# Both down layers of a fused kernel: seven block products in place of eight

## The chip, the cores and the metric

The kernel runs on one core of a Trainium2 chip. Its time is the device time in microseconds (us), the median of three runs. TensorE (PE in the profile) multiplies, with its weight loads (PEld) beside it; VectorE (DVE), ScalarE (ACT) and GpSimd (POOL) do the elementwise work; SyncE (SP) issues the DMAs. A weight is kept as a high and a low fp32r part (two numbers whose sum is the fp32 value), so one block product over one tile of 128 rows is three matmuls: high by high, low by high, high by low.

## The reference, cut to what matters

```python
def _moe2_ref(x, w1, w2, w3, w_out):
    a = x @ w1                  # 1792 x 1024, x is 1792 x 768
    b = x @ w2
    h = a * b @ w3              # w3: 1024 x 1024
    return h @ w_out            # w_out: 1024 x 768

def reference(...):
    attn_out = sigmoid attention  # 4 batches, 12 heads, 448 x 64
    x = attn_out as 1792 x 768
    x = _moe_ref(x, ...)          # RMS norm, SiLU gate: 768 -> 1536 -> 768
    return _moe2_ref(x, w1, w2, w3, w_out)
```

## The kernel before, in words

The kernel works on the four batches of 448 tokens; a matmul has 128x128 weights and 448 token columns. The last quarter of its program is what matters here. It goes through these stages, `g` being a pair of batches: gate layer of pair 1 (`a_winograd`), first down layer of pair 1 (`b_units(1)`), then for pair 0 and for pair 1 the product layer (`c_winograd`, `a * b`) and the last down layer (`d_units`). The weights of the last down layer, `w3 @ w_out`, were multiplied together early in the program (`w3o_group`) and lie in DRAM as `w3o`, eight row tiles of 128 x 768.

**The product layer** computes `x @ w1` and `x @ w2` for both batches of a pair with seven block products in place of eight: `winograd` (L531). The right-hand blocks are seven combinations `w0` to `w6` of the layer's input, made by `right_blocks` (L497): four subtractions on DVE, then for each of the seven blocks a rounding copy on ACT and a subtraction on DVE (`split2`, L319). `y_blocks` (L523) loads four input tiles (`ys`) from DRAM and makes the seven blocks of one of three slices k. The left-hand blocks are made for each m by `winograd_blocks` (L159): four DVE subtractions of 128x384, of which the last (L170) and the next set's first (L166) wait for POOL to have read the buffer `s`; then `split_weight` makes the two parts of each block with an ACT copy (L131) and a POOL subtraction (L134). Blocks lie in a ring of four `ws` tiles, two blocks each. Each of the seven products of an m is nine matmuls (three slices, three runs) into one of four PSUM banks (`ps_w`), and DVE adds it to the others: L548 frees the bank of product 1, L550 that of product 2, and so on; product 0's is freed by an ACT copy (L546). Bank j is needed again four products later. For each of the eight m and both batches, `c_winograd` (L573) multiplies the two results on DVE (L575) and splits the product (`ab`).

**The last down layer** (`d_group`, L627) has 12 groups for each pair (six m, two batches); a group sums 24 matmuls (eight row tiles, three runs) in a bank of `ps_m`, ACT copies it out (L631) and SP stores it (L632). Its weights come as twelve `wf` tiles of 128x512 with one ACT copy and one POOL subtraction each. Beside pair 0's groups three `y_blocks(1, k)` run for pair 1's product layer, the last of them after the eighth of twelve groups.

A scheduler fixes the order of the instructions on each engine; each engine runs its own list in that order, so a waiting instruction holds all behind it on its engine.

Of the kernel before, what the change touches and what calls it, by code (L numbers as in the profile page):

```python
# [44 lines left out]
def fused_kernel(ctx: ExitStack, tc: tile.TileContext, qkv, wg, wv, wo, w1, w2, w3, wo2, gam, out):  # L45
# [90 lines left out]
    class Weights:  # L136
# [13 lines left out]

        def add_winograd(self, srcs):

            first = len(self.seq)
            for n in range(len(srcs) * 7 // 2):
                m = [(2 * n + j) // 7 for j in range(2) if (2 * n + j) % 7 == 0]
                self.add(srcs[m[0]] if m else None, None)
            return first

        def winograd_blocks(self):  # L159

            while True:
                f = self.loaded.pop(0)
                a11, a12, a21, a22 = (f[:, j, k * WH : (k + 1) * WH] for j in range(2) for k in range(2))
                s = wp.tile([P, WT], F32, tag="mag", bufs=1, name="s")
                s1, s2 = s[:, :WH], s[:, WH:]
# [12 lines left out]
        def load_to(self, n):  # L178
            while self.n_load <= min(n, len(self.seq) - 1):
                src, kt, double, keep, use = self.seq[self.n_load]  # L180
                t = None
                if src is not None:
                    if self.out == 2:
                        return
                    self.out += 1
                    if kt is None:
                        t = wp.tile([P, 2, WT], F32, tag="wd", bufs=2, name="wd")
                        for j in range(2):
                            nc.sync.dma_start(out=t[:, j, :].rearrange("p (k c) -> p k c", c=P), in_=src[j])
                        self.loaded.append(t)  # L190
                    elif double:
                        t = load_double(src, kt)
                    else:
                        t = wp.tile([P, WT], F32, tag="wf", bufs=2, name="wf")
                        nc.sync.dma_start(out=t[:, : kt * P].rearrange("p (k c) -> p k c", c=P), in_=src)
                self.raw[self.n_load] = t
                self.n_load += 1

        def split_to(self, n):

            n = min(n, len(self.seq) - 1)
            while self.n_split <= n and len(self.split) < self.BUFS:
# [3 lines left out]
                f = self.raw.pop(i)  # L206
                w = WT if kt is None else kt * P
                if double:
# [11 lines left out]
                if kt is None:  # L220
# [35 lines left out]

    def add_d():
        return [
            [W.add(w3o[4 * h : 4 * h + 4, :, m * P : (m + 1) * P].rearrange("k p c -> p k c"), 4) for h in range(2)]
            for m in range(KD)  # L260
        ]

# [31 lines left out]
    i_c = add_gated(("w1", "w2"), KF2, 2)  # L294
    i_d = add_d()
    i_c2 = add_gated(("w1", "w2"), KF2)
    i_d2 = add_d()

# [42 lines left out]
    NH = DM // 2  # L341

    def w3o_group(kt, nh):
        ps = psm()[:, :NH]
# [5 lines left out]
        nc.scalar.activation(o, ps, AF.Copy)  # L350
        nc.sync.dma_start(out=w3o[kt, :, nh * NH : (nh + 1) * NH], in_=o)

# [77 lines left out]
    def take_out(p):  # L430
# [65 lines left out]

    def right_blocks(k, b11, b12, b21, b22):  # L497

        tt = nc.vector.tensor_tensor

        def put(j, bl, src):
            t = acts["w", j, k] = right_tile(f"w{j}", bl)
            split2(t, src)
# [19 lines left out]
    def y_blocks(g, k):  # L523
        y = []
        for m in (k, k + 3):
            for b in range(2):
                y.append(scratch("ys"))
                nc.sync.dma_start(out=y[-1], in_=yd.pop((g, b, m)))
        right_blocks(k, *y)

    def winograd(first, m, done):  # L531

        tt = nc.vector.tensor_tensor

        def product(j):
            n = 7 * (m % 2) + j
            i = first[m // 2] + n // 2
            t = W.get(i)[:, :, n % 2 * WH : (n % 2 + 1) * WH]
            ps = ps_w.tile([P, 512], F32, tag="w", bufs=4, name="w")[:, :S]
            runs(ps, t, 0, [acts["w", j, k] for k in range(3)], True, True)  # L540
            W.split_to(i + 3)
            return ps

        u, v, c11, c21 = (scratch(n) for n in ("u", "v", "c11", "c21"))
# [18 lines left out]
    def a_winograd(m):  # L563
# [7 lines left out]
        winograd(i_a2, m, done)  # L571

    def c_winograd(first, m):  # L573
# [52 lines left out]

    def d_group(g, m, b):  # L627
        t = [(W.get(i), 4) for i in (i_d2 if g else i_d)[m]]
        ps = accumulate(t, [acts["ab", b, k] for k in range(KF2)])
        o = scratch("o")  # L630
        nc.scalar.activation(o, ps, AF.Copy)  # L631
        nc.sync.dma_start(out=out[m * P : (m + 1) * P, (2 * g + b) * S : (2 * g + b + 1) * S], in_=o)  # L632

    def a_units():
# [10 lines left out]
    def d_units(g):  # L645
        for m in range(KD):
            for b in range(2):
                yield 4.5, (lambda m=m, b=b: d_group(g, m, b)), (i_d2 if g else i_d)[m][1]

# [182 lines left out]
```

## Time and profile before

| | us |
|---|---|
| median of three runs (1090.33 to 1092.02) | 1091.6 |
| profiled execution | 1088.77 |
| its span, first to last instruction | 1086.8 |
| product layer, pair 0 (from 760.21) | 102.8 |
| last down layer, pair 0 (from 863.03) | 58.8 |
| product layer, pair 1 (from 921.87) | 102.7 |
| last down layer, pair 1 (from 1024.57, its matmuls) | 58.7 |

The span is what the instructions cover; some 2 us of the execution lie around it. The stages are read off TensorE's own timeline, where one row covers a run of like matmuls; a stage's length is the distance from its first matmul to that of the next stage.

### The profile page before, as it was taken

Reading aid. Unit: us, or ns where it says so; the run is one execution under the profiler, and the core shown is the slowest. Engines: PE = TensorE matmul, PEld = TensorE weight load, DVE = VectorE, ACT = ScalarE, POOL = GpSimd, SP = SyncE. Lnnn points to the kernel's source line nnn. Section 1 sums busy time; section 2 is a strip of 40 time slices with the busy share of each in tenths; the row PEclk is TensorE's granted clock in tenths of the full one; section 3 lists DMA queues with packets and bytes.
Section 4 is the critical chain, followed back from the end, with each engine's and each line's share of the span. In section 5 each row is a group of like instructions: output and inputs, shape, how many; then the busy total and the mean of one; then the engine's idle time right before and its main releaser. Section 6 shows DMA issues by size and latency. Waiting matters only on the chain.

```text
span 1086.8 us, 13929 instructions
## 1 busy us (share of the span) xinstructions
PE 1069.4 (98%) x5152; PEld 900.2 (83%) x5152; DVE 776.9 (71%) x1018; ACT 390.2 (36%) x708; POOL 469.3 (43%) x382
## 2 busy tenths in 40 slices
PE   9999899998999999999999999999999999999998
PEld 4338799996766676799999999999999999999997
DVE  5998998999456578569787778677787635787500
ACT  5673211112244333214544443133433244333221
POOL 2646254443223323333656554223665434656420
PEclk9999899999999999999999999999999999999999
DMA  7733455575345367663221113766311244210131
GB/s 255 259 132 117 143 177 181 181 270 177 124 160 172 111 247 254 228 225 123 78 82 62 59 59 102 263 243 207 100 64 59 68 159 130 80 59 30 48 101 51
DMA packets 60980, 153.22 MB, mean 141 GB/s; under 512 B 5872, under 2 KB 32624, under 8 KB 60912
## 3 DMA queue, kind: packets, MB, share of 16 engines
q1 hardware_dynamic: 60912, 152.33, 41.7%
q8 instruction: 41, 0.67, 0.3%
q14 instruction: 27, 0.22, 0.1%
HBM read 114.95 MB, written 37.36 MB: 140 GB/s over the span
## 4 chain that ended last, share of the span: by engine, by line
PE 70%; DVE 5%; DMA 3%; ACT 1%; issue 0%; POOL 0%; SPq 0%; DVEq 0%; ACTq 0%
PE w L307 32%; PE psm L307 32%; PE av L414 2%; PE sc L396 1%; DMA raw<-in_qkv 1%; DVE mag L112 1%; PE psm L384 1%; PE av L410 1%; DVE wf L121 1%; DVE wf L124 1%; DVE mag L111 1%; PE psm L396 1%; DMA wd<-in_wg 1%; DVE wf L113 0%; DMA wd<-in_wv 0%; DMA wd<-in_wo 0%
## 5 line engine op out<-in xcount | busy, mean ns | idle before, releaser
L307 PE MATMUL w<-w,ws 128*128 128x448 f32 x1764 | 360.4, 366 | 0.1
L307 PEld LDWEIGHTS w<-w,ws 128*128 128x128 f32 x1764 | 331.2, 188 | 28.8 <-DVE c L550 0.5
L134 POOL TENSOR_TENSOR ws<-wf,ws 128x768 fp32r<-128x768 f32 (+1 forms) x88 | 153.3, 1743 | 133.8 <-ACT ws L131 129.5
L307 PE MATMUL psm<-hm,ws 128*128 128x448 f32 x864 | 178.1, 367 | 0.0
L307 PEld LDWEIGHTS psm<-hm,ws 128*128 128x128 f32 x864 | 162.0, 188 | 16.8 <-issue 1.7
L134 POOL TENSOR_TENSOR ws<-wd,ws 128x384 fp32r<-128x384 f32 x112 | 123.9, 1118 | 102.7 <-ACT ws L131 93.9
L307 PE MATMUL psm<-x,ws 128*128 128x448 f32 x648 | 140.4, 376 | 6.2 <-POOL ws L133 5.1
L307 PEld LDWEIGHTS psm<-x,ws 128*128 128x128 f32 x648 | 124.0, 193 | 24.0 <-POOL ws L133 5.5
L134 POOL TENSOR_TENSOR ws<-s,ws 128x384 fp32r<-128x384 f32 x84 | 94.8, 1136 | 67.6 <-ACT ws L131 67.6
L133 POOL CAST ws<-wf 128x768 fp32r<-128x768 f32 (+1 forms) x52 | 45.2, 869 | 180.8 <-PE psm L307 85.8
L307 PE MATMUL psm<-ab,ws 128*128 128x448 f32 x576 | 117.7, 366 | 0.0
L307 PEld LDWEIGHTS psm<-ab,ws 128*128 128x128 f32 x576 | 108.2, 188 | 9.2
L121 DVE SCALAR_TENSOR_TENSOR wf<-wd,wf 128x768 uint32<-128x768 uint32 (+1 forms) x76 | 90.2, 1186 | 2.5
L113 DVE TENSOR_SCALAR wf<-mag 128x768 uint32<-128x768 uint32 (+1 forms) x76 | 66.3, 872 | 34.6 <-POOL ws L134 30.6
L111 DVE TENSOR_SCALAR mag<-wd 128x768 uint32<-128x768 uint32 (+1 forms) x76 | 55.7, 733 | 36.8 <-DMA wd<-in_wo 22.6
L131 ACT ACTIVATE ws<-wd 128x384 fp32r<-128x384 f32 x112 | 54.8, 515 | 71.2 <-PE w L307 48.0
L124 DVE SCALAR_TENSOR_TENSOR wf<-wd,wf 128x768 uint32<-128x768 uint32 (+1 forms) x76 | 74.2, 976 | 1.5
L307 PE MATMUL psm<-o,ws 128*128 128x384 f32 x384 | 68.8, 339 | 0.0
L307 PEld LDWEIGHTS psm<-o,ws 128*128 128x128 f32 x384 | 67.4, 188 | 1.2 <-issue 1.1
L112 DVE TENSOR_SCALAR mag<-mag 128x768 f32<-128x768 f32 (+1 forms) x76 | 66.5, 874 | 1.7
L321 ACT ACTIVATE hm<-s 128x448 fp32r<-128x448 f32 x48 | 27.6, 576 | 93.3 <-DVE s L606 70.7
L414 PE MATMUL av<-a,raw 128*64 128x448 f32 x288 | 59.4, 548 | 0.0
(96 smaller groups left out, 1124.5 us busy)
## 6 DMA issues: line engine op xcount, KB each, us to landing
raw<-in_qkv SPq DMA_DIRECT2D x23, 736.0 KB, 5.8
wd<-in_wo SPq DMA_DIRECT2D x20, 768.0 KB, 6.1
wd<-in_w SPq DMA_DIRECT2D x16, 768.0 KB, 5.2
wd<-w SPq DMA_DIRECT2D x32, 384.0 KB, 3.6
wd<-in_wg SPq DMA_DIRECT2D x12, 768.0 KB, 4.5
wd<-in_wv SPq DMA_DIRECT2D x12, 768.0 KB, 4.8
wd<-in_w SPq DMA_DIRECT2D x16, 512.0 KB, 4.3
w<-wf SPq DMA_DIRECT2D x16, 384.0 KB, 2.7
```

The costliest lines, as they stand in the source:

```text
L111: nc.vector.tensor_scalar(out=mag.bitcast(U32), in0=hi, scalar1=0x7FFFFFFF, scalar2=None, op0=ALU.bitwise_and)
L112: nc.vector.tensor_scalar(out=mag, in0=mag, scalar1=HI_MIN, scalar2=HI_MAX, op0=ALU.max, op1=ALU.min)
L113: nc.vector.tensor_scalar(out=u, in0=mag.bitcast(U32), scalar1=3, scalar2=0x3FFFFFFF, op0=ALU.logical_shift_left, op1=ALU.bitwise_and,)
L121: nc.vector.scalar_tensor_tensor(out=u, in0=hi, scalar=0xC0000000, in1=u, op0=ALU.bitwise_and, op1=ALU.bitwise_or)
L124: nc.vector.scalar_tensor_tensor(out=u, in0=lo, scalar=29, in1=u, op0=ALU.logical_shift_right, op1=ALU.bitwise_or)
L131: nc.scalar.activation(t[:, 0, :w], f[:, :w], AF.Copy)
L133: nc.gpsimd.tensor_copy(out=t[:, 0, :w], in_=f[:, :w])
L134: nc.gpsimd.tensor_tensor(out=t[:, 1, :w], in0=f[:, :w], in1=t[:, 0, :w], op=ALU.subtract)
L307: nc.tensor.matmul(ps, w, xt[:, xi, :], start=first and r == 0 and j == 0, stop=last and r == 2 and j == n - 1)
L321: i = nc.scalar.activation(dst[:, 0, :], src, AF.Copy)
L396: nc.tensor.matmul(ps[j], r[d, k], r[d, Q0 : Q0 + S], start=True, stop=True)
L414: nc.tensor.matmul(av[p][d, :], r[:, v + j * D : v + (j + 1) * D], a[:, j, :], start=False, stop=(c == 2))
```

## The change

The last down layer is computed like the product layer, from seven block products. For two output tiles m = 2n, 2n+1 the left-hand blocks are combinations of quarters of `w3o`; the split of the sum is into even and odd row tiles, so `w3o_row` stores the row tiles in another order. `d_winograd` runs seven products over the eight row tiles in two halves of four (`D_HALVES`); a part is six matmuls (two slices, three runs). The sums of all seven products stay in PSUM over both halves, in the four banks of `ps_w` and the three of `ps_m`, and the second half's products are combined as in the product layer (`combine`, cut out of `winograd`) and stored from DVE's results. A weight tile holds three blocks of 128x256.

`c_winograd` no longer splits its products: it keeps those of two m (`held`) and every second m gives them to `right_blocks`, which makes seven blocks of the down layer's input. That is 28 blocks of two parts for a pair, in place of 16; 24 lie in the tiles that `ab` had, and four in places of the product layer's own input blocks (`ab_tile`). The three `y_blocks(1, n)` that refill these places stand between the two halves of each n, the last between the halves of the last n. The tiles `acc`, `r` and `ys` share four buffers with the kept products (`held`), where `ys` had been among the six scratch buffers. So the loads of `ys` move up in SP's list: in pair 1's first down layer the first two stand ahead of a weight load (`wf` from `wo`) that used to come long before them, and two more stand ahead of the gate layer's third pair of weight loads (`wd` from `wg` and `wv`).

```diff
+    def held(name):
+        return scr.tile([P, S], F32, tag="held", bufs=4, name=name)
...
-        def add_winograd(self, srcs):
+        def add_winograd(self, srcs, per=2):
...
-            for n in range(len(srcs) * 7 // 2):
-                m = [(2 * n + j) // 7 for j in range(2) if (2 * n + j) % 7 == 0]
-                self.add(srcs[m[0]] if m else None, None)
+            for n in range(len(srcs) * 7 // per):
+                m = [(per * n + j) // 7 for j in range(per) if (per * n + j) % 7 == 0]
+                self.add(srcs[m[0]] if m else None, -per)
...
-                t = parts(wp, "ws", self.BUFS, "ws", WT, STEP)
-                self.split[i] = [t, 2]
+                self.split[i] = [t, max(2, -kt)]
...
-                    for j in range(2):
+                if kt < 0:
+                    for j in range(-kt):
                         s = self.made.pop(0) if self.made else next(self.blocks)
-                        split_weight(t[:, :, j * WH : (j + 1) * WH], s, WH)
+                        split_weight(t[:, :, j * w : (j + 1) * w], s, w)
...
+    D_HALVES = [(n, h) for n, hs in enumerate(((0, 1), (1, 0), (1, 0))) for h in hs]
+
+    def add_d_winograd():
+        return W.add_winograd([[d_rows(2 * n + j, h) for j in range(2)] for n, h in D_HALVES], 3)
...
+    def w3o_row(kt):
+        return kt // 4 * 4 + kt % 2 * 2 + kt % 4 // 2
...
-            acc[b] = scr.tile([P, S], F32, tag="acc", bufs=2, name="acc")
+            acc[b] = held("acc")
...
-        r = rms[b] = scr.tile([P, S], F32, tag="r", bufs=2, name="r")
+        r = rms[b] = held("r")
...
+    def ab_tile(name, n):
+        if n < 2 * KF1:
+            return h_tile(name, n // 2)
+        return right_tile(name, (n - 2 * KF1) // 2)
...
-                y.append(scratch("ys"))
+                y.append(held("ys"))
...
+    def d_winograd(g, first, n, between=None):
+        ps = [bank() if j < 4 else psm()[:, :S] for j in range(7)]
+        def part(e, j):
+            i, c = divmod(7 * e + j, 3)
+            t = W.get(first + i)[:, :, c * 2 * P : (c + 1) * 2 * P]
+            h = D_HALVES[e][1]
+            runs(ps[j], t, 0, [acts["d", j, 2 * h + k] for k in range(2)], e == 2 * n, e > 2 * n)
+            W.split_to(first + i + 3)
+            W.load_to(first + i + 6)
+            return ps[j]
+        def done(b, *rows):
+            for j, o in enumerate(rows):
+                m = 2 * n + j
+                nc.sync.dma_start(out=out[m * P : (m + 1) * P, (2 * g + b) * S : (2 * g + b + 1) * S], in_=o)
+        for j in range(7):
+            part(2 * n, j)
+        if between:
+            between()
+        combine(lambda j: part(2 * n + 1, j), done)
...
     def c_winograd(first, m):
         def done(b, x, y):
-            nc.vector.tensor_tensor(out=y, in0=x, in1=y, op=ALU.mult)
-            acts["ab", b, m] = t = h_tile("ab", m)
-            split2(t, y)
+            t = ab[m % 2, b] = held("ab")
+            nc.vector.tensor_tensor(out=t, in0=x, in1=y, op=ALU.mult)
         winograd(first, m, done)
+        if m % 2:
+            right_blocks(m // 2, ab[0, 0], ab[0, 1], ab[1, 0], ab[1, 1], True)
...
-    for j, u in enumerate(d_units(0)):
-        run(u)
-        if j in (1, 4, 7):
-            y_blocks(1, j // 3)
+    for n in range(KD // 2):
+        d_winograd(0, i_d, n, lambda: y_blocks(1, n))
     for m in range(KF2):
         c_winograd(i_c2, m)
-    for u in d_units(1):
-        run(u)
+    for n in range(KD // 2):
+        d_winograd(1, i_d2, n)
```

Two places show how the engines' lists change. On DVE, in pair 0's product layer, from the last sum of an odd m to the first sums of the next: `v`, `u` and the `c` tiles are the product layer's sums, `s` and `wd` the weight blocks, `t_` a combination and `w_` a split block. Before:

```order
L560 TENSOR_TENSOR v<-w,v 128x448
L575 TENSOR_TENSOR u<-v,u 128x448
L166 TENSOR_TENSOR s<-wd 128x384
L167 TENSOR_TENSOR s<-s,wd 128x384
L326 TENSOR_TENSOR ab<-u,ab 128x448
L168 TENSOR_TENSOR wd<-wd 128x384
L548 TENSOR_TENSOR v<-w,u 128x448
L170 TENSOR_TENSOR s<-wd,s 128x384
L550 TENSOR_TENSOR c_6564<-w,u 128x448
```

And now:

```order
L607 TENSOR_TENSOR v<-w,v 128x448
L169 TENSOR_TENSOR s<-wd 128x384
L625 TENSOR_TENSOR ab<-v,u 128x448
L170 TENSOR_TENSOR s<-s,wd 128x384
L527 TENSOR_TENSOR t_6554<-ab,t_6554 128x448
L529 TENSOR_TENSOR ab<-ab 128x448
L531 TENSOR_TENSOR ab<-ab,t_6554 128x448
L333 TENSOR_TENSOR w_6566<-t_6554,w_6566 128x448
L333 TENSOR_TENSOR w_6570<-ab,w_6570 128x448
L333 TENSOR_TENSOR w_6574<-ab,w_6574 128x448
L333 TENSOR_TENSOR w_6577<-ab,w_6577 128x448
L171 TENSOR_TENSOR wd<-wd 128x384
```

Between the last sum of the old m (L560, now L607) and the first of the new (L548, now L595, which is the next row of the changed list) stood five instructions; now eleven stand there. The added ones are the combinations and splits of `right_blocks`.

On DVE, at the end of pair 0's last down layer, the last `y_blocks` (`ys`, `t_`, `w_`) and the sums behind it. Before, the stage ended with the splits of that `y_blocks` alone:

```order
L510 TENSOR_TENSOR t_7582<-ys,t_7582 128x448
L512 TENSOR_TENSOR ys<-ys 128x448
L514 TENSOR_TENSOR ys<-ys,t_7582 128x448
L326 TENSOR_TENSOR w_7594<-t_7582,w_7594 128x448
L326 TENSOR_TENSOR w_7598<-ys,w_7598 128x448
L326 TENSOR_TENSOR w_7602<-ys,w_7602 128x448
L326 TENSOR_TENSOR w_7605<-ys,w_7605 128x448
```

And now:

```order
L333 TENSOR_TENSOR w_7806<-ys,w_7806 128x448
L173 TENSOR_TENSOR s<-wd,s 128x384
L333 TENSOR_TENSOR w_7813<-ys,w_7813 128x448
L333 TENSOR_TENSOR w_7810<-t_7805,w_7810 128x448
L333 TENSOR_TENSOR w_7828<-ys,w_7828 128x448
L527 TENSOR_TENSOR t_7805<-ys,t_7805 128x448
L531 TENSOR_TENSOR ys<-ys,t_7805 128x448
L595 TENSOR_TENSOR v<-w,u 128x448
L333 TENSOR_TENSOR w_7817<-t_7805,w_7817 128x448
L333 TENSOR_TENSOR w_7821<-ys,w_7821 128x448
L333 TENSOR_TENSOR w_7825<-ys,w_7825 128x448
L597 TENSOR_TENSOR c_7833<-w,u 128x448
```

The same splits now stand among the weight blocks of the next product layer (`s`) and ahead of the sums of the last two output tiles (`c`, `v`).

## Rows read from the trace of the kernel before

**Rows 1.** The page: busy time, share of the span and instructions.

```profile
span 1086.8 us, 13929 instructions
...
PE 1069.4 (98%) x5152; PEld 900.2 (83%) x5152; DVE 776.9 (71%) x1018; ACT 390.2 (36%) x708; POOL 469.3 (43%) x382
```

**Rows 2.** Timeline of PE: start us, us, engine, line, operation, tiles, count.

```profile
517.57 127.73 PE L307 MATMUL w<-w,ws 128*128 128x448 f32 x624
...
760.21 102.99 PE L307 MATMUL w<-w,ws 128*128 128x448 f32 x504
863.03 59.00 PE L307 MATMUL psm<-ab,ws 128*128 128x448 f32 x288
921.87 102.86 PE L307 MATMUL w<-w,ws 128*128 128x448 f32 x504
1024.57 58.73 PE L307 MATMUL psm<-ab,ws 128*128 128x448 f32 x288
```

**Rows 3.** Windows: busy us of each engine, clock, DMA; the last four stages.

```profile
core 0: us, PE busy (x) PEld busy (x) DVE busy (x) ACT busy (x) POOL busy (x), PEclk, DMA share, GB/s
760.00:863.00 103.00, 103.00 (x506) 94.77 (x505) 78.69 (x120) 39.77 (x83) 60.65 (x56) 1.00 0.22 72
863.00:922.00 59.00, 59.00 (x290) 54.27 (x290) 25.62 (x38) 24.53 (x48) 21.14 (x15) 1.00 0.42 135
922.00:1024.50 102.50, 102.50 (x505) 94.51 (x504) 76.34 (x113) 37.94 (x77) 59.48 (x54) 1.00 0.16 54
1024.50:1086.80 62.30, 58.80 (x290) 53.93 (x288) 2.35 (x4) 12.35 (x22) 11.97 (x9) 1.00 0.24 79
```

**Rows 4.** Groups on DVE, pair 1's product layer: count | busy, mean ns | idle before, releaser.

```profile
L170 DVE TENSOR_TENSOR s<-wd,s 128x384 f32<-128x384 f32 x7 | 9.5, 1354 | 5.9 <-POOL ws L134 5.9
L166 DVE TENSOR_TENSOR s<-wd 128x384 f32<-128x384 f32 x7 | 7.1, 1021 | 10.2 <-POOL ws L134 10.2
L326 DVE TENSOR_TENSOR ab<-c,ab 128x448 fp32r<-128x448 f32 x8 | 6.3, 784 | 0.1
```

**Rows 5.** Groups on ACT in the same stage.

```profile
L131 ACT ACTIVATE ws<-wd 128x384 fp32r<-128x384 f32 x28 | 13.8, 515 | 19.8 <-PE w L307 10.7 <-DVE s L170 6.8 <-POOL ws L134 2.3
```

**Rows 6.** Timeline, pair 1's product layer, DVE and POOL around the end of an m.

```profile
948.33 0.62 DVE L560 TENSOR_TENSOR v<-w,v 128x448 f32<-128x448 f32 x1
...
951.71 0.62 DVE L326 TENSOR_TENSOR ab<-u,ab 128x448 fp32r<-128x448 f32 x1
...
952.25 0.55 DVE L168 TENSOR_TENSOR wd<-wd 128x384 f32<-128x384 f32 x1
...
952.72 0.62 DVE L548 TENSOR_TENSOR v<-w,u 128x448 f32<-128x448 f32 x1
953.63 1.01 POOL L134 TENSOR_TENSOR ws<-wd,ws 128x384 fp32r<-128x384 f32 x1
```

**Rows 7.** Timeline of POOL: a subtraction of 128x512.

```profile
1015.25 1.29 POOL L134 TENSOR_TENSOR ws<-wf,ws 128x512 fp32r<-128x512 f32 x1 [2.12 <-ACT ws L131]
```

**Rows 8.** Timeline, last down layer of pair 0: first DVE, then POOL.

```profile
912.57 4.17 DVE L326 TENSOR_TENSOR w<-ys,w 128x448 fp32r<-128x448 f32 x3
...
912.14 1.39 POOL L134 TENSOR_TENSOR ws<-wd,ws 128x384 fp32r<-128x384 f32 x1 [7.19 <-DVE ys L514]
913.49 1.40 POOL L134 TENSOR_TENSOR ws<-s,ws 128x384 fp32r<-128x384 f32 x1
```

**Rows 9.** The same stage, an earlier place: DVE, then POOL.

```profile
882.75 1.70 DVE L326 TENSOR_TENSOR w<-ys,w 128x448 fp32r<-128x448 f32 x3
...
882.44 4.39 POOL L134 TENSOR_TENSOR ws<-wf,ws 128x512 fp32r<-128x512 f32 x2 [6.98 <-ACT ws L131]
```

**Rows 10.** Instructions of line 476: duration ns min/median/max, first and last start.

```profile
L476 DVE SCALAR_TENSOR_TENSOR xs<-xs,g_sb,r x12: 673/684/1440, 488.9 to 513.8; 128x448 f32<-128x448 f32 x12
```

**Rows 11.** The end: timeline of ACT, and the outputs' DMAs.

```profile
1083.38 0.54 ACT L631 ACTIVATE o<-psm 128x448 f32<-128x448 f32 x1 [4.32 <-PE psm L307]
...
DMA to landing us min/median/max: 1.9/2.0/5.0
```

More of the change, by code (lines that the diff above doesn't have):

```diff
@@ L161, in winograd_blocks @@
             while True:
-                f = self.loaded.pop(0)
-                a11, a12, a21, a22 = (f[:, j, k * WH : (k + 1) * WH] for j in range(2) for k in range(2))
+                f, w = self.loaded.pop(0)
+                a11, a12, a21, a22 = (f[:, j, k * w : (k + 1) * w] for j in range(2) for k in range(2))
                 s = wp.tile([P, WT], F32, tag="mag", bufs=1, name="s")
-                s1, s2 = s[:, :WH], s[:, WH:]
+                s1, s2 = s[:, :w], s[:, w : 2 * w]
                 nc.vector.tensor_tensor(out=s1, in0=a21, in1=a22, op=ALU.add)
@@ L185, in load_to @@
                     self.out += 1
-                    if kt is None:
+                    if kt < 0:
                         t = wp.tile([P, 2, WT], F32, tag="wd", bufs=2, name="wd")
+                        w = WT // -kt
                         for j in range(2):
-                            nc.sync.dma_start(out=t[:, j, :].rearrange("p (k c) -> p k c", c=P), in_=src[j])
-                        self.loaded.append(t)
+                            d = t[:, j, : 2 * w].rearrange("p (k c) -> p k c", c=P)
+                            nc.sync.dma_start(out=d, in_=src[j])
+                        self.loaded.append((t, w))
                     elif double:
@@ L206, in split_to @@
                 f = self.raw.pop(i)
-                w = WT if kt is None else kt * P
+                w = WT // -kt if kt < 0 else kt * P
                 if double:
@@ L255, in add_moe, with d_rows @@
         return W.add(src[m][:, 6 * h : 6 * h + 6, :], 6, True, d)
[L257 to L261, printed above, removed]
+    def d_rows(m, h):
+        return w3o[4 * h : 4 * h + 4, :, m * P : (m + 1) * P].rearrange("k p c -> p k c")
+    D_HALVES = [(n, h) for n, hs in enumerate(((0, 1), (1, 0), (1, 0))) for h in hs]
+    def add_d_winograd():
+        return W.add_winograd([[d_rows(2 * n + j, h) for j in range(2)] for n, h in D_HALVES], 3)
     ahead = [(n, w, m) for m in range(KF2) for n, w in (("w1", w1), ("w2", w2))]
@@ L294, in fused_kernel @@
     i_c = add_gated(("w1", "w2"), KF2, 2)
-    i_d = add_d()
+    i_d = add_d_winograd()
     i_c2 = add_gated(("w1", "w2"), KF2)
-    i_d2 = add_d()
+    i_d2 = add_d_winograd()
     RUNS = ((0, 0), (1, 0), (0, 1))
@@ L350, in w3o_group @@
         nc.scalar.activation(o, ps, AF.Copy)
-        nc.sync.dma_start(out=w3o[kt, :, nh * NH : (nh + 1) * NH], in_=o)
+        nc.sync.dma_start(out=w3o[w3o_row(kt), :, nh * NH : (nh + 1) * NH], in_=o)
     A1 = dict(raw=3, a=5, al=2, xr=9, wd=2)
@@ L495, in right_tile, with right_blocks @@
         return parts(p, f"x{bl}", n, name, step=step)
-    def right_blocks(k, b11, b12, b21, b22):
+    def ab_tile(name, n):
+        if n < 2 * KF1:
+            return h_tile(name, n // 2)
+        return right_tile(name, (n - 2 * KF1) // 2)
+    def right_blocks(k, b11, b12, b21, b22, down=False):
         tt = nc.vector.tensor_tensor
         def put(j, bl, src):
-            t = acts["w", j, k] = right_tile(f"w{j}", bl)
+            t = acts["d" if down else "w", j, k] = ab_tile(f"w{j}", 7 * k + j) if down else right_tile(f"w{j}", bl)
             split2(t, src)
@@ L526, in y_blocks, with bank @@
             for b in range(2):
-                y.append(scratch("ys"))
+                y.append(held("ys"))
                 nc.sync.dma_start(out=y[-1], in_=yd.pop((g, b, m)))
         right_blocks(k, *y)
+    def bank():
+        return ps_w.tile([P, 512], F32, tag="w", bufs=4, name="w")[:, :S]
     def winograd(first, m, done):
-        tt = nc.vector.tensor_tensor
         def product(j):
@@ L538, in product @@
             t = W.get(i)[:, :, n % 2 * WH : (n % 2 + 1) * WH]
-            ps = ps_w.tile([P, 512], F32, tag="w", bufs=4, name="w")[:, :S]
+            ps = bank()
             runs(ps, t, 0, [acts["w", j, k] for k in range(3)], True, True)
@@ L542, in product, with combine @@
             return ps
+        combine(product, done)
+    def d_winograd(g, first, n, between=None):
[17 more added lines that the diff above has]
+        combine(lambda j: part(2 * n + 1, j), done)
+    def combine(product, done):
+        tt = nc.vector.tensor_tensor
         u, v, c11, c21 = (scratch(n) for n in ("u", "v", "c11", "c21"))
@@ L625, in b_group @@
         nc.sync.dma_start(out=d, in_=y)
[L627 to L632, printed above, removed]
     def a_units():
@@ L643, in b_units @@
                 yield 6.8, (lambda m=m, b=b: b_group(g, m, b)), (i_b2 if g else i_b)[m][1]
[L645 to L648, printed above, removed]
     def run(unit, more=0):
```

3 lines of the change are left out of this document (2 added, 1 removed).

## The prediction

> **What bounds the kernel now.** I read the page first: TensorE is busy for 98% of the span, DVE for 71% and POOL for 43% [rows 1]. Then TensorE's timeline over the last quarter [rows 2]: four long rows follow each other with no idle time noted between them, so the stages that the change touches end when their matmuls end. The product layers take 102.82 us from the first matmul to the next stage's (760.21 to 863.03) for 504 matmuls, 0.2040 us each; pair 0's last down layer takes 58.84 us for 288, 0.2043 us each. The granted clock is 1.00 in all four stages [rows 3]. So a matmul taken away is worth 0.204 us as long as the other engines keep up, and the third view asks whether they do: in the windows DVE is busy for 76.3 of pair 1's 102.5 us in the product layer and POOL for 59.5; in the down layers DVE has 25.6 of 59.0 us and 2.4 of 62.3 [rows 3]. The stage with little room is thus the product layer, and the change puts work on DVE there.
>
> **Matmuls taken away.** Three n, seven products, four slices and three runs are 252 matmuls per pair in place of 288: 72 fewer in all. 72 x 0.2043 = **14.7 us** less. A part of six lasts 1.23 us, a half of 42 lasts 8.58, a down layer 51.5; a product of nine in the product layer lasts 1.84 us and an m 12.85.
>
> **Work added on DVE, product layer.** Per two m, the change takes away four splits and adds seven, and adds four combinations: seven more DVE instructions, 28 per stage. Three in a row take 1.70 us, so one follows another after (1.70 - 0.62) / 2 = 0.54 us [rows 9]; among POOL's work their mean is 0.784 [rows 4]. 28 x 0.54 = 15.1 us, 28 x 0.784 = 22.0 us: DVE comes to 91 to 98 us of the 102.8. It fits, without room for 16.1 us of standing behind POOL that the stage has now (5.9 before L170, 10.2 before L166 [rows 4]); that idle time shrinks when DVE arrives later, and what remains of it is a rival below.
>
> The place where it shows first is the end of an odd m, where eleven instructions now stand ahead of the first sum of the next m, where there were five. In the trace L560 starts at 948.33 and the L548 behind the five at 952.72: six steps in 4.39 us, 0.73 each [rows 6]. Twelve steps would take 8.8 us, and the sum itself 0.62: 9.4 us. TensorE needs that bank again five products after the old m ended, 5 x 1.84 = 9.2 us. So it waits for about 0.3 us; at 0.54 a step (7.1 us in all) for nothing; and if five POOL subtractions get in between, each 1.39 - 0.54 = 0.85 more (below), for about 2.2. I take 0.5, nearer to the step that this very place shows. There are three such ends per stage (the fourth leads into the down layer, whose first half fills seven banks without a sum): 6 x 0.5 = 3 us, with ends of 0 and 13.
>
> **POOL and DVE together.** Down weights come in 42 blocks of 128x256 per pair, not 12 of 128x512. POOL took 1.01 us alone for 384 columns [rows 6] and 1.29 for 512 [rows 7], so an estimate from those two rows is 0.73 for 256; DVE took 0.55 for 384 and 0.62 for 448 [rows 6], so about 0.41 for 256. Now the rows that show the two engines side by side: three DVE splits take 4.17 us when POOL has a queue, 1.39 each, and POOL's subtractions beside them 1.39 and 1.40 each [rows 8]; where DVE was already running, its three take 1.70 and POOL's two of 512 columns stretch to 4.39 [rows 9]. They take turns: a DVE instruction with two SBUF inputs and a POOL subtraction do not overlap, and one of each costs 1.39 us, 0.85 of what they take alone (1.01 + 0.62 = 1.63). Per two m of the product layer the taking of turns then covers 14 POOL subtractions, 8 weight subtractions and 15 other DVE instructions: 14 x 1.01 + 8 x 0.55 + 15 x 0.62 = 27.8 us alone, x 0.85 = 23.7 of 25.7. In pair 0's down layer, per n: 14 x 0.73 + 8 x 0.41 + 11 x 0.62 = 20.3, x 0.85 = 17.3 of 17.2. The first fits, the second just: bounds are 0 and (20.3 - 17.2) x 3 = 9.3 us. I take 1 us, since the weight ring is ahead there: ACT's copies mostly wait for TensorE to give a tile back (10.7 of 19.8 us [rows 5]), so POOL may run late before TensorE does.
>
> The Trainium skill, SBUF — State Buffer, section "SBUF: two separate sides", says that GpSimd and a VectorE op with two SBUF inputs share one port pair as an exclusive lock held for the whole instruction. The rows agree that the two exclude each other; that each holds it for its whole duration they don't (1.39, not 1.63). By the rule's letter the sum would be the slower rival's below.
>
> **The last `y_blocks`.** It had four of twelve groups behind it, 4 x 24 x 0.2043 = 19.6 us of TensorE's work; now it has one half, 8.58. DVE's list holds there 11 instructions of `y_blocks`, four weight subtractions and seven sums: 11 x 0.54 + 4 x 0.55 + 7 x 0.62 = 12.5 us, and the block that is split last but for two is wanted one product (1.84 us) after the half. 12.5 - 8.6 - 1.8 = 2.1 us late if none of it starts early, 0 if some does. I take 1.
>
> **The rest.** The end: the last matmul is now followed by a DVE sum (0.62 [rows 6]) and not by an ACT copy (0.54 [rows 11]), then by a DMA of the same size (2.0 us to land [rows 11]): +0.1. Sums of the down layer: 7 x 0.62 = 4.3 us per n on a DVE that pair 1 leaves free. SP: the early `ys` loads wait for `r`, whose last reader starts at 513.8 [rows 10]; the weights behind them are for the gate layer's third m, 517.57 [rows 2] + 2 x 12.85 = 543.3, 29 us later. Nothing, and if that cover were gone it would be the load's few us once. ACT gains three copies per two m on 37.9 of 102.5 us [rows 3]: nothing.
>
> **Sum.** 1086.8 - 14.7 + 0.1 + 3 + 1 + 1 = 1077.2 of span. Around the span lay 1088.77 - 1086.8 = 2.0 us: 1079.2 for an execution like the profiled one. The median of the runs is 1091.6 - 1088.8 = 2.8 above that one: **1082.0**.
>
> **Rivals.**
> - *No new waits.* DVE bursts run at 0.54 a step and the idle time behind POOL gives way: 1091.6 - 14.7 + 0.1 = 1077.0. For it: DVE and POOL have room on paper. Against: twelve steps at the place above went at 0.73.
> - *DVE's order becomes the bound.* If the 16.1 us behind POOL stay and the 28 instructions cost 0.54, DVE needs 76.3 + 15.1 + 16.1 = 107.5 in each product layer, 4.7 more than its matmuls: 1077.0 + 9.4 = 1086.4. At 0.784 each it is 114.4, 11.6 more: 1100.2. Between them lies the point of no change, at 0.63 each. For it: L166 and L170 wait in order, ahead of sums that free banks. Against: they wait because DVE is early.
> - *Slower: the shared turn.* If POOL and DVE exclude each other for their full durations, a pair of m needs 27.8 us in place of 25.7 (eight pairs: 16.8) and an n of pair 0 20.3 in place of 17.2 (three: 9.3): 1077.0 + 26.1 = 1103.1. It begins to cost at a factor of 0.93 on the durations (25.7 / 27.8), and at 0.96 nothing is left of the gain (8 x 26.7 + 3 x 19.5 = 272, 15 over the 257 of eight pairs and three n). For it: DVE instructions of 1354 and 1021 ns mean in place of 0.55 [rows 4]. Against: 1.39 in place of 1.63 [rows 8].
> - *The change doesn't do what it says.* The lists show 72 matmuls fewer; no chance is given to it.
>
> **Chances.** Forecast, with waits of 2 to 9 us (1079 to 1086): 0.50. No new waits (1075.5 to 1079): 0.18. DVE's order, its lower end (1086 to 1089.4): 0.11; its middle (within 0.2%, 1089.4 to 1093.8, about what a measurement can tell from no change): 0.08. Slower, by the shared turn or the upper end of DVE's order: 0.13. So faster 0.79, same 0.08, slower 0.13. The range goes from 1076 (no waits, and 1.0 for the spread of the runs) to 1090, where about 2 in 10 lie outside.
>
> **What would show it.** Right: TensorE's row of the down layers shrinks to about 51.5 us each, the product layers grow by 1 to 3 us each, with waits on DVE's L595 or L597 at odd ends, and DVE's busy time there is above 90 us. The third rival would show as POOL and DVE means that both rise by half, with TensorE waiting on POOL's L137. The second: idle time on DVE in front of L169 and L173 that has not shrunk. It is wrong altogether if TensorE's matmuls run at another pitch than 0.204 us when six and not 24 go to one bank in a row.

## The result, and the profile after

The changed kernel takes 1097.84 us (median of seven runs, 1094.69 to 1100.33) against 1091.6 for the kernel before, also of seven runs: a ratio of 1.0067, with a 95% interval of 1.0051 to 1.0084. It is slower by 0.7%, and the forecast of 1082.0, with a range of 1076 to 1090, was wrong. The profiled execution took 1098.54 us, its span is 1096.8.

First the page: busy time, share of the span and instructions of each engine, which answers to [rows 1].

```profile
span 1096.8 us, 14136 instructions
...
PE 1063.5 (97%) x5080; PEld 888.9 (81%) x5080; DVE 869.3 (79%) x1164; ACT 406.2 (37%) x774; POOL 515.2 (47%) x442
```

The 72 matmuls are gone (5152 to 5080), DVE is busy for 92 us more and POOL for 46. Next TensorE's timeline over the last quarter, which answers to [rows 2]: start, us, line, operation, tiles, count, and in brackets the idle time before the row and what released it.

```profile
763.66 35.03 PE L314 MATMUL w<-w,ws 128*128 128x448 f32 x171
800.44 26.34 PE L314 MATMUL w<-w,ws 128*128 128x448 f32 x126 [1.75 <-DVE v L595]
828.65 27.49 PE L314 MATMUL w<-w,ws 128*128 128x448 f32 x126 [1.87 <-DVE v L595]
857.89 21.67 PE L314 MATMUL w<-w,ws 128*128 128x448 f32 x105 [1.75 <-DVE v L595]
...
895.90 3.96 PE L314 MATMUL w<-w,ws 128*128 128x448 f32 x18 [2.93 <-DVE v L595]
...
929.27 11.24 PE L314 MATMUL w<-w,ws 128*128 128x448 f32 x54
941.08 11.47 PE L314 MATMUL w<-w,ws 128*128 128x448 f32 x54 [0.57 <-DVE c L597]
952.80 13.08 PE L314 MATMUL w<-w,ws 128*128 128x448 f32 x63 [0.25 <-DVE v L595]
967.65 26.32 PE L314 MATMUL w<-w,ws 128*128 128x448 f32 x126 [1.77 <-DVE v L595]
995.81 27.52 PE L314 MATMUL w<-w,ws 128*128 128x448 f32 x126 [1.83 <-DVE v L595]
1025.09 21.65 PE L314 MATMUL w<-w,ws 128*128 128x448 f32 x105 [1.76 <-DVE v L595]
```

The long unbroken rows of before are cut at every odd end: six waits of 1.75 to 1.87 us in the product layers, one of 2.93 in pair 0's down layer, 0.57 and 0.25 at the start of pair 1's product layer, all on the first two sums of an m or an n (L595, L597). The stages, which answer to [rows 3] (busy time of each engine, instructions in brackets, then TensorE's granted clock and the DMA):

```profile
763.66:874.50 110.84, 105.39 (x505) 95.64 (x504) 93.93 (x137) 43.16 (x91) 68.06 (x61) 0.98 0.19 61
874.50:929.27 54.77, 51.84 (x254) 47.16 (x253) 50.87 (x81) 25.96 (x64) 34.69 (x37) 1.00 0.45 139
929.27:1041.70 112.43, 106.11 (x506) 95.28 (x505) 98.11 (x147) 44.16 (x95) 67.89 (x61) 0.98 0.20 65
1041.70:1096.80 55.10, 51.51 (x253) 47.13 (x251) 32.64 (x53) 15.43 (x41) 27.43 (x34) 0.99 0.24 79
```

| stage, us | before | after | difference |
|---|---|---|---|
| product layer, pair 0 | 102.8 | 110.8 | +8.0 |
| last down layer, pair 0 | 58.8 | 54.8 | -4.0 |
| product layer, pair 1 | 102.7 | 112.4 | +9.7 |
| last down layer, pair 1 (matmuls) | 58.7 | 51.5 | -7.2 |

Together +6.5, close to the 6.2 between the two medians. The profiled spans differ by 10.0: the remaining 3.5 lie ahead of 760 us. They aren't put down to the change, since variants below with the same code there began this product layer between 758.2 and 764.9.

The matmuls still go at 0.204 us (171 in 35.03), except in one stretch of each product layer, behind the wait at its second odd end. A window at that place, same columns:

```profile
829.00:833.00 4.00, 4.00 (x14) 3.60 (x13) 3.86 (x7) 0.95 (x3) 2.12 (x2) 0.57 0.20 39
```

A mean of 0.57 between two levels is the clock at 1.2 GHz for most of these 4 us; 14 matmuls run where 19.6 would fit, and the row of 126 above takes 27.49 us, where rows of 126 without a stop take 25.96 (e8 below): 1.5 us more. The other long row, 26.34, is clear of the slow clock; it has a short stop in it, 0.35 us at an even end (813.67).

Why L595 is late is read from DVE's timeline at the first odd end, with POOL's behind it:

```profile
785.88 0.63 DVE L601 TENSOR_TENSOR c<-w,u 128x448 f32<-128x448 f32 x1 [0.99 <-PE w L314]
786.42 0.61 DVE L524 TENSOR_TENSOR t<-ab 128x448 f32<-128x448 f32 x1
786.95 1.44 DVE L625 TENSOR_TENSOR ab<-c,c 128x448 f32<-128x448 f32 x1
788.31 1.44 DVE L333 TENSOR_TENSOR w<-t,w 128x448 fp32r<-128x448 f32 x1
789.67 0.61 DVE L604 TENSOR_TENSOR u<-w,u 128x448 f32<-128x448 f32 x1
...
791.62 0.61 DVE L607 TENSOR_TENSOR v<-w,v 128x448 f32<-128x448 f32 x1
...
796.07 3.32 DVE L333 TENSOR_TENSOR w<-ab,w 128x448 fp32r<-128x448 f32 x3
799.31 0.55 DVE L171 TENSOR_TENSOR wd<-wd 128x384 f32<-128x384 f32 x1
799.77 0.61 DVE L595 TENSOR_TENSOR v<-w,u 128x448 f32<-128x448 f32 x1
```

```profile
786.54 1.37 POOL L137 TENSOR_TENSOR ws<-wd,ws 128x384 fp32r<-128x384 f32 x1 [1.58 <-ACT ws L134]
787.87 1.40 POOL L137 TENSOR_TENSOR ws<-s,ws 128x384 fp32r<-128x384 f32 x1
...
791.18 1.40 POOL L137 TENSOR_TENSOR ws<-wd,ws 128x384 fp32r<-128x384 f32 x1
```

At L601 DVE is still early: it has waited 0.99 us for TensorE. From there to the start of L595 stand 19 instructions, seven up to L607 and twelve from it, in 799.77 - 785.88 = 13.89 us, 0.73 each. TensorE has seven products to do before it wants the bank, 7 x 1.84 = 12.9 us. DVE is done at 800.38, TensorE goes on at 800.44.

This count holds at three of the six odd ends. Over both product layers and the down layer between them DVE waited for TensorE by more than 0.2 us at three places only: at 785.88, at 843.32 and at 1010.51, and from each of them the 19 instructions take 13.9 us. The row gives the total, the number and the longest:

```profile
DVE c L601 <- PE w L314: 3.4, 3, 1.2
```

At the other three odd ends DVE had not caught up since an earlier place, so it brought the lateness along. There its own list sets the pace, with its waits for POOL: 13.6 us of them in pair 0's product layer, 10.7 in pair 1's.

### The profile page after: what moved, and what is told of

It is laid out like the page before. It is cut to its first block, busy times and chain, and to the rows that moved or that the text cites. A ratio compares the mean times of both kernels' runs of the same rounds, so it can differ in the third digit from the quotient of the medians.

```text
span 1096.8 us, 14136 instructions
## 1 busy us (share of the span) xinstructions
PE 1063.5 (97%) x5080; PEld 888.9 (81%) x5080; DVE 869.3 (79%) x1164; ACT 406.2 (37%) x774; POOL 515.2 (47%) x442
## 5 line engine op out<-in xcount | busy, mean ns | idle before, releaser
L314 PE MATMUL w<-w,ws 128*128 128x448 f32 x2052 | 427.2, 368 | 15.2 <-DVE v L595 13.9
L314 PEld LDWEIGHTS w<-w,ws 128*128 128x128 f32 x2052 | 386.6, 189 | 53.7 <-DVE v L595 18.1
L137 POOL TENSOR_TENSOR ws<-wd,ws 128x384 fp32r<-128x384 f32 (+1 forms) x160 | 169.0, 1070 | 93.8 <-ACT ws L134 92.2
L137 POOL TENSOR_TENSOR ws<-s,ws 128x384 fp32r<-128x384 f32 (+1 forms) x120 | 129.6, 1088 | 115.6 <-ACT ws L134 82.4
L137 POOL TENSOR_TENSOR ws<-wf,ws 128x768 fp32r<-128x768 f32 (+1 forms) x64 | 119.8, 1872 | 61.8 <-ACT ws L134 57.6
L134 ACT ACTIVATE ws<-wd 128x384 fp32r<-128x384 f32 (+1 forms) x160 | 73.0, 482 | 70.1 <-PE w L314 49.2
L134 ACT ACTIVATE ws<-s 128x384 fp32r<-128x384 f32 (+1 forms) x120 | 56.3, 483 | 64.7 <-DVE s L170 46.7
L115 DVE TENSOR_SCALAR mag<-mag 128x768 f32<-128x768 f32 (+1 forms) x76 | 68.7, 904 | 1.7
L169 DVE TENSOR_TENSOR s<-wd 128x384 f32<-128x384 f32 (+1 forms) x40 | 35.7, 892 | 38.9 <-POOL ws L137 37.1
L457 POOL TENSOR_TENSOR acc<-acc,sq 128x448 f32<-128x448 f32 x20 | 27.3, 1365 | 71.1 <-ACT sq L456 62.3
```

Source lines behind the costliest of these rows:

```text
L115: nc.vector.tensor_scalar(out=mag, in0=mag, scalar1=HI_MIN, scalar2=HI_MAX, op0=ALU.max, op1=ALU.min)
L134: nc.scalar.activation(t[:, 0, :w], f[:, :w], AF.Copy)
L137: nc.gpsimd.tensor_tensor(out=t[:, 1, :w], in0=f[:, :w], in1=t[:, 0, :w], op=ALU.subtract)
L314: nc.tensor.matmul(ps, w, xt[:, xi, :], start=first and r == 0 and j == 0, stop=last and r == 2 and j == n - 1)
L457: nc.gpsimd.tensor_tensor(out=acc[b], in0=acc[b], in1=sq, op=ALU.add)
```

## The experiments

Two theories of the lost time stood against each other. **Order**: each engine works its list in turn, the four banks allow DVE a lateness of less than three products, and the burst at an odd end is longer than that. **Turns**: DVE's instructions with two SBUF inputs and POOL's subtractions exclude each other, and the stage has too much of both. The kernel before, run beside them, had medians of 1089.56, 1090.85 and 1091.29 in the three sessions (e1 to e4, e5 to e8, e9 and e10).

### e1: seven banks, put in the wrong layer

```diff
-            ps = bank()
+            ps = bank() if j < banks else psm()[:, :S]
```

> The product layers spread their seven products over seven PSUM banks (four of ps_w, three of ps_m) in place of four; every engine's list keeps the order of the changed kernel. Theory A, the order of DVE's list: at each odd end DVE comes to the next m's first sums 1.9 us after their bank is wanted, but has the time back later in the pair; with seven banks the six waits of 1.9 to 2.0 us go, and the two stretches of half clock behind them (1.5 us each) too: 14 to 15 us less than the changed kernel's 1097.8, so about 1083. Theory B, DVE's throughput: DVE cannot do a pair's work in the 25.7 us that TensorE needs, the banks only put the wait off: at most 5 us less, 1093 or more. The wait of 3.1 us in pair 0's down layer stays under both.

The number of banks was handed over the wrong way round (`banks` counts the products that go to `ps_w`; the others take the three banks of `ps_m`): the gate layer got seven, the product layers kept four. 1098.23 us, ratio 1.0073 (1.0049 to 1.0098), stages and waits as in the changed kernel. It says only that the gate layer has no use for more banks; the question went to e5.

### e2: POOL's subtractions out of the last four stages

```diff
+        if not low:
+            nc.scalar.activation(t[:, 1, :w], f[:, :w], AF.Copy, scale=2.0**-13)
+            return
         nc.gpsimd.tensor_tensor(out=t[:, 1, :w], in0=f[:, :w], in1=t[:, 0, :w], op=ALU.subtract)
```

> From the first product layer of the last quarter on, the low part of a weight block is a scaled copy on ACT in place of the subtraction on POOL (so the low part's value is left out); DVE's list is the changed kernel's but for what the scheduler moves. Theory A with turns taken with POOL as its cause: DVE steps fall to 0.54 us, DVE is no longer late at the odd ends, all waits there go: about 1083, and the 3.1 us in the down layer shrink. Theory A by the mere number of instructions: DVE's lateness of 2.3 us at an odd end stays, 12 steps of 0.54 and a sum make 7.1 in place of 8.8 us, the waits shrink from 1.95 to about 0.3: 1086. Theory B, throughput, gives 1083 too; a result above 1093 would clear POOL altogether.

1075.24 us, ratio 0.9862 (0.9836 to 0.9888): 14.3 us under the kernel before. The same four stages by windows:

```profile
759.92:862.70 102.78, 102.78 (x505) 94.57 (x504) 75.40 (x140) 66.33 (x152) 0.00 (x0) 1.00 0.21 67
862.70:914.11 51.41, 51.41 (x255) 47.38 (x254) 43.02 (x86) 40.58 (x107) 0.00 (x0) 1.00 0.51 158
914.11:1016.85 102.74, 102.74 (x506) 94.61 (x505) 76.24 (x142) 66.03 (x150) 0.00 (x0) 1.00 0.20 65
```

TensorE doesn't wait in these stages, although DVE's list holds the same 19 instructions at the first odd end, one split two places later. These are the rows of L601 and L595, three lines further down here:

```profile
782.14 0.62 DVE L604 TENSOR_TENSOR c<-w,u 128x448 f32<-128x448 f32 x1 [1.21 <-PE w L317]
...
792.65 0.61 DVE L598 TENSOR_TENSOR v<-w,u 128x448 f32<-128x448 f32 x1
```

The 19 take 10.51 us, 0.55 each and not 0.73. DVE's busy time falls from 93.9 and 98.1 us to 75.4 and 76.2: about 20 us of DVE's time in each product layer of the changed kernel are its turns with POOL. It shows too that the new order of `w3o`, the lent places, the new end and, but for POOL's part in them, the narrow weight blocks cost nothing: 72 matmuls give their 14.7 us, within 0.4, where DVE keeps up.

### e3: four splits per two m in place of the seven blocks

```diff
-            right_blocks(m // 2, ab[0, 0], ab[0, 1], ab[1, 0], ab[1, 1], True)
+            k = m // 2
+            for j in range(4):
+                t = acts["d", j, k] = ab_tile(f"w{j}", 7 * k + j)
+                split2(t, ab[j // 2, j % 2])
+            for j in range(4, 7):
+                acts["d", j, k] = acts["d", j - 4, k]
```

> The product layer makes no seven blocks of its products: it only splits the four kept tiles every second m, and the down layer's blocks 4 to 6 read those of 0 to 2 again (so the combinations are left out and the outputs differ). The down layer's 252 matmuls and its weight blocks stay. All theories: the six waits at odd ends go, since DVE has four splits there and not eleven instructions; what stays is the down layer's own cost. If 72 matmuls are worth 14.7 us and only the right-hand blocks eat them: 1091.6 - 14.7 + 3 (the wait in pair 0's down layer) = 1080. If the narrower weight blocks cost too, above 1084.

1075.36 us, ratio 0.9862 (0.9840 to 0.9884). Here POOL keeps all its work (66.3 and 67.6 us in the product layers) and DVE is at 79.1 and 82.7; no wait at the odd ends, 0.8 us in all of pair 0's down layer. Taking the seven instructions away is as good as taking POOL away, so neither alone is the cause: it is the added instructions at the price that they have beside POOL.

### e4: the first two `y_blocks` behind the sums of their n

```diff
-        if between:
+        if between and n == 2:
             between()
         combine(lambda j: part(2 * n + 1, j), done)
+        if between and n < 2:
+            between()
```

> The first two y_blocks of pair 0's down layer are made after the sums of their n and not between its halves; the last stays. Theory A, order: the wait of 3.1 us for the sum L595 that stood behind the first y_blocks goes, nothing else changes: 1097.8 - 3 = 1095, with the six waits at odd ends as they were. If the wait was only DVE being full there (rival), it comes back as a wait at the start of the next product layer: 1097 to 1099.

1099.7 us, ratio 1.0095 (1.0064 to 1.0127). The wait of 2.9 us in pair 0's down layer goes, and comes back as 1.10 and 4.31 us at the start of pair 1's product layer, where the sums of the last n now stand behind two `y_blocks` in DVE's list:

```profile
922.34 2.10 PE L314 MATMUL w<-w,ws 128*128 128x448 f32 x9 [1.10 <-ACT u L595]
928.75 35.68 PE L314 MATMUL w<-w,ws 128*128 128x448 f32 x162 [4.31 <-DVE v L597]
```

### e5: seven banks in the product layers

The edit of e1, with seven banks in `c_winograd` and four in the gate layer.

> The seven PSUM banks now in the product layers of the last quarter (the run before had given them to the gate layer, so its question stayed open); DVE's list keeps the changed kernel's order. Theory A, lateness at one place: DVE is late only at odd ends and has the time back within the pair, so the six waits of 1.95 us and the slow stretches go: about 1083. Theory B, throughput: with the work of DVE and POOL taking turns, a pair needs more than 25.7 us; the first wait of each stage moves back by a few products, and each pair loses about 1.3 us all the same: 1093 to 1098.

1090.06 us, ratio 1.0001 (0.9978 to 1.0023), between the two forecasts. The product layers come to 103.7 and 103.9 us, but pair 0's down layer takes 61.7 in place of 54.8. Pair 1's takes 54.6 in place of 51.5. The lateness hasn't gone: DVE carries it past the odd ends into the next stage, where the row behind the largest wait is this:

```profile
888.73 6.11 PE L314 MATMUL w<-w,ws 128*128 128x448 f32 x18 [4.54 <-DVE v L595]
```

### e6: the blocks given out as steps behind the sums of the next m

`right_steps` is `right_blocks` as a generator of seven steps, and `step` takes the next of them.

```diff
-            right_blocks(m // 2, ab[0, 0], ab[0, 1], ab[1, 0], ab[1, 1], True)
+            steps_left.append(right_steps(m // 2, ab[0, 0], ab[0, 1], ab[1, 0], ab[1, 1]))
+            if m == KF2 - 1:
+                while steps_left:
+                    step()
...
         tt(out=v, in0=p6, in1=u, op=ALU.add)
+        step()
+        step()
```

(Two more steps follow the sum into `c11` and three the first one into `u`.)

> The blocks of two m's products are made between the first sums of the next m, two or three steps after each of them, and not ahead of them; nothing is added or left out, four banks as in the changed kernel. Theory A: bank 1 is freed 11 DVE steps earlier, the waits at odd ends fall from 1.95 us to under 0.5: 1084 to 1087. Theory B: the waits move to the sums behind the steps (banks 2 to 4), their total stays above 8 us: 1093 or more.

1089.12 us, ratio 0.9991 (0.9971 to 1.0011), between the two forecasts; product layers of 106.8 and 108.5 us. The odd ends wait less at L628 (the line of L595 here), but wait at the sum behind the steps:

```profile
803.44 25.96 PE L314 MATMUL w<-w,ws 128*128 128x448 f32 x126 [0.51 <-DVE c L641]
831.06 7.60 PE L314 MATMUL w<-w,ws 128*128 128x448 f32 x36 [1.66 <-DVE c L641]
```

### e7: steps and seven banks together

The edits of e5 and e6.

> Spread steps and seven banks in the product layers together: DVE may be up to 11 us late before TensorE waits. Theory A: no wait left in the product layers, 1082 or less (only the 3.1 us in pair 0's down layer stay). Theory B: DVE's lateness grows by the same amount each pair, TensorE waits at the end of each stage: 1090 or more.

1081.6 us (1078.32 to 1085.75), ratio 0.9917 (0.9896 to 0.9938): this version computes all that the changed kernel does and beats both kernels. Windows of pair 0's product layer, three stretches of its down layer, and pair 1's product layer:

```profile
758.16:860.99 102.83, 102.83 (x505) 94.61 (x504) 93.47 (x134) 41.69 (x89) 68.76 (x61) 1.00 0.19 60
860.99:884.26 23.27, 18.73 (x92) 16.63 (x90) 22.64 (x36) 12.63 (x30) 13.90 (x15) 0.97 0.45 126
884.26:890.48 6.22, 6.22 (x18) 5.61 (x19) 6.22 (x12) 2.03 (x5) 5.17 (x6) 0.57 0.51 175
890.48:919.84 29.36, 29.36 (x145) 27.04 (x144) 25.41 (x41) 14.78 (x35) 17.51 (x19) 1.00 0.44 142
919.84:1022.57 102.73, 102.73 (x505) 94.59 (x504) 96.12 (x141) 41.29 (x88) 68.97 (x61) 1.00 0.21 67
```

The product layers are back at 102.8 us without a wait while DVE is busy for 93.5 and 96.1 of them, beside 69 of POOL's. So the added work fits the stage, turns included; what didn't fit was a burst of it ahead of a sum that frees one of four banks. DVE's waits for POOL gave way too: 2.7 us in pair 1's product layer, 10.7 in the changed kernel. One wait of 4.54 us and the slow stretch behind it (18 matmuls in 6.22) are left, in pair 0's down layer.

### e8: a quarter of POOL's subtractions given to DVE

```diff
+        e = nc.gpsimd if pool else nc.vector
-        nc.gpsimd.tensor_tensor(out=t[:, 1, :w], in0=f[:, :w], in1=t[:, 0, :w], op=ALU.subtract)
+        e.tensor_tensor(out=t[:, 1, :w], in0=f[:, :w], in1=t[:, 0, :w], op=ALU.subtract)
```

(`pool` is false for 14 of the 56 blocks of a product layer; the rest is as in the changed kernel.)

> In each product layer of the last quarter 14 of the 56 low parts of weight blocks are subtracted by DVE (0.47 us each) and not by POOL (about 0.9 in turns). If DVE's own time is what is short: 14 x 0.47 = 6.6 us more per stage, 1105 or more. If the turn that DVE and POOL take is what is short: 14 x 0.45 = 6.3 us less of it per stage, 1087 or less. If it is the order alone: within 3 us of 1097.8.

1091.15 us, ratio 0.9994 (0.9971 to 1.0016), 6.7 us under the changed kernel and none of the three times forecast. DVE does more itself (98.7 us of pair 0's product layer), POOL 15 us less (53.2), and the waits at the odd ends fall to between 1.2 and 1.6 us. DVE's waits for POOL over the two product layers and the down layer between them were these in the changed kernel, first those in total, then their number and the longest:

```profile
DVE s L169 <- POOL ws L137: 21.1, 11, 3.8
DVE s L173 <- POOL ws L137: 9.0, 10, 1.9
```

and are these here:

```profile
DVE s L170 <- POOL ws L138: 4.9, 4, 2.2
DVE s L174 <- POOL ws L138: 2.8, 3, 1.2
```

### e9 and e10: `y_blocks` as steps too, and with less on POOL

e9 is e7 with this edit, which gives out the blocks of the first two `y_blocks` of pair 1 in the same way; e10 is e9 with the edit of e8.

```diff
-        right_blocks(k, *y)
+        if g and k < 2:
+            steps_left.append(right_steps(k, *y, False))
+        else:
+            right_blocks(k, *y)
```

> The run with both the spread steps and seven banks, and with the blocks of the first two y_blocks of pair 1 also given out as steps behind the sums of their n, so that they stand behind and not ahead of the first sum. Theory (order in DVE's list against the slack of the banks): the one wait that was left, 4.7 us before the second half of the first n, goes, and with it the stretch at half clock behind it (2.5 us); pair 0's down layer takes 51.3 to 53 us in place of 58.8, the product layers stay at 102.8, and the time is 1074 to 1077 us. Rival (DVE has no more time to give, so that the wait only moves): the blocks come late at the start of pair 1's product layer, its waits there are 3 to 6 us, and the time stays at 1080 to 1083.

1083.79 us, ratio 0.9947 (0.9926 to 0.9968), no better than e7 (0.9917). From the start of pair 0's product layer to the end the two profiles are alike (319.4 and 319.6 us); e9's came to that layer 3.7 us later. The rival was right that the wait only moves, but not on where: it stays in the down layer, at later sums (L645, L649).

```profile
889.98 1.47 PE L314 MATMUL psm<-w,ws 128*128 128x448 f32 x6 [2.90 <-DVE c L645]
892.59 4.01 PE L314 MATMUL psm<-w,ws 128*128 128x448 f32 x12 [1.14 <-DVE v L649]
```

> The same, and 14 of the 56 weight subtractions of each product layer moved from POOL to DVE. Theory (with the order mended, the turns with POOL fit beside TensorE): nothing to win, within 2 us of the run without the move. Rival (the wait for POOL's turn still costs): if the run without the move still shows waits in the product layers, this one is 2 to 5 us faster; and if DVE itself is at its limit, the five us that it took on per stage make it 2 to 8 us slower.

1091.71 us, ratio 1.0014 (0.9996 to 1.0033), 7.9 us more than e9. The down layer of pair 0 in e9, then in this run:

```profile
864.64:923.05 58.41, 53.93 (x253) 47.98 (x252) 54.15 (x85) 27.77 (x67) 36.26 (x38) 0.97 0.45 141
```

```profile
867.00:928.35 61.35, 56.59 (x253) 48.49 (x252) 58.25 (x92) 29.36 (x71) 37.88 (x41) 0.94 0.44 136
```

DVE is busy for 54.2 and 58.3 us where the matmuls take 51.4, and for 43.0 in e2. With work left over for DVE, neither of the two sequences tried (e7, e9) fits this stage, and more work on DVE makes it longer. Once the order of the product layers is mended, the shift that won 6.7 us in e8 loses.

## Why the prediction was wrong, point by point

**Matmuls taken away, -14.7: right.** Pair 1's down layer takes 51.5 us; e2 and e3 lie 14.3 and 14.2 under the kernel before.

**Odd ends, 6 x 0.5 = 3: the step that failed.** Each costs 1.75 to 1.87 us by the rows, 10.7 together, and the slow stretch behind the second of each stage 1.5 more. The price of a step was right (0.73 forecast; 0.73 measured over 19), and so were the twelve steps: with the sum they take 8.8 us (791.62 to 800.38) where 9.4 were forecast. What failed is where the count began: "Twelve steps would take 8.8 us" starts at the last sum of the old m and takes it to be on time. L607 begins at 791.62, and TensorE had ended the old m at 763.66 + 126 x 0.204 = 789.4: 2.3 us late, against 0.8 at the place of [rows 6] (948.33, after 921.87 + 126 x 0.204 = 947.6). The 2.3 and the 8.8 make 11.0 against 9.2. Among the sums of the old m the kernel before had a product and a split:

```profile
944.73 0.63 DVE L575 TENSOR_TENSOR c<-c,c 128x448 f32<-128x448 f32 x1
...
946.45 1.24 DVE L326 TENSOR_TENSOR ab<-c,ab 128x448 fp32r<-128x448 f32 x1
```

The change adds a combination and one more split there (L524, L333), and beside POOL the product and the first split take 1.44 each. Counted from the last place at which DVE waits for TensorE, L601, it is 19 x 0.73 + 0.61 = 14.5 us against 12.9: 1.6 late. In the changed kernel's list on DVE those rows stand a few lines above the twelve. The sum also had no term for lateness carried from one odd end to the next.

**POOL and DVE together, +1 in pair 0's down layer (0 to 9.3): too small.** The working had 17.3 us of turns in 17.2 per n, and then took 1 because TensorE seldom has to wait for weights. It did not wait for weights: it waited 2.9 us for a sum that stood behind `y_blocks` in DVE's list, and the stage is 3.3 us longer than its matmuls. With the product layers mended (e7, e9) the stage is 7 us longer than its matmuls, nearer to the upper end.

**The last `y_blocks`, +1 (0 to 2.1): right in size**, 0.57 and 0.25 at the start of pair 1's product layer, 1.7 with the slower matmuls around these stops. The forecast had TensorE waiting for a block; it waited for sums (L597, L595).

**The rest, 0.1: right**; e2 leaves no room for more.

**The rivals.** *DVE's order* was the one that came, in the upper half of its 1086.4 to 1100.2: it gave each product layer 107.5 to 114.4 us, the trace shows 110.8 and 112.4, and pair 1's DVE is busy for 98.1 and waits 10.7 for POOL, which leaves little of the stage. The argument against it ("they wait because DVE is early") was too strong: the 16.1 us of such waiting [rows 4] fell to 10.7 while DVE was late, not to nothing. The rival's sum is no fixed bound either, as e7's 2.7 us show. It had 0.19 of the chances and a share of the 0.13 given to a slower kernel, and the time fell in the latter; the point of no change that it named, 0.63 us for an added instruction, lay between the two prices on the table, and the measured price is (98.11 - 76.34) / 28 = 0.78. *The shared turn* as full exclusion didn't come: TensorE never waited for POOL's L137 there, and e7 fits 93 to 96 us of DVE and 69 of POOL into 102.8. *No new waits* is what e2 and e3 show, where the burst or the turns are gone.

Taken from start to start of the matmuls, the product layers' loss is whole. Pair 0's +8.0 are three odd ends of 2.0 to 2.1 us (a wait and some 0.3 us in the matmuls around it), the slow stretch of 1.5 and the stop of 0.35. Pair 1's +9.7 are three odd ends, 6.2 together, the slow stretch of 1.5, a stop of 0.4 at an even end (980.89) and the 1.7 at the start. So the odd ends, with what they brought along, took 16 us where the sum had 3: 13 of the 15.8 by which the time was missed.

What stays open is how the 54 us of DVE in pair 0's down layer could be brought below 51.

## What to carry to other kernels

An added burst on an engine that works in order is to be counted from the last instruction at which that engine still waits for the bottleneck, not from the place where the burst seems to begin, and where it doesn't wait between two bursts the lateness adds up; against it stands the work that the bottleneck does until it needs the first buffer back. Price the steps at what they cost beside the engine that they exclude, and ask of every idle time whether it ends sooner if the engine comes later. Here more buffers alone moved such a lateness to the next stage, and a better order alone moved much of it to the next sum; only both together let the product layers run at the pace of their matmuls.

## What the runs showed of the hardware

**The turns cost DVE a fifth of its time.** In the timeline above the sums with one operand in PSUM (L601, L604, L607) take 0.61 to 0.63 us, L607 beside POOL's row at 791.18 as well, and L625 and L333, with two operands in SBUF, 1.44 each beside POOL's 1.37 and 1.40. The splits of pair 1's product layer (count, busy us, mean ns) in the changed kernel:

```profile
L333 DVE TENSOR_TENSOR w<-ab,w 128x448 fp32r<-128x448 f32 x16 | 15.2, 980 | 0.0
```

and without POOL (e2, where the lines are three further down):

```profile
L336 DVE TENSOR_TENSOR w<-ab,w 128x448 fp32r<-128x448 f32 x16 | 9.4, 619 | 0.1
```

The Trainium skill, SBUF — State Buffer, section "SBUF: two separate sides", names VectorE ops with two SBUF inputs as ones that exclude a GpSimd op which reads SBUF. The splits, and the sums from PSUM that stay at 0.61, agree with that.

**The clock falls after some waits and not after others.** In the changed kernel 2.93 us of waiting in pair 0's down layer were followed by 18 matmuls in 3.96 us (the row at 895.90 above), in e8 the same wait by 18 in 5.46:

```profile
892.65 5.46 PE L315 MATMUL w<-w,ws 128*128 128x448 f32 x18 [2.93 <-DVE v L596]
```

After the waits of 4.54 us in e5 and e7 the clock fell in both (6.11 and 6.39 us for 18), at the odd ends of the changed kernel only after the second of each product layer, and in e4 only after that of pair 1, though its waits were as long. What decides it the runs don't show; it made a wait dearer by 1.5 to 2.5 us in the places named.
